# Attention with sinks and a feed-forward network on one core: the order of all engines from a list scheduler in the source, and probabilities transposed by VectorE and DMA

## The chip, the core and the metric

The kernel runs on one core of a Trainium2 chip. A core has TensorE (PE; its weight loads are shown apart as PEld), VectorE (DVE), ScalarE (ACT), GpSimd (POOL) and SyncE (SP), which here issues every DMA. Each engine executes its own instructions strictly in order and waits on semaphores for the others. The metric is the device time of one execution in microseconds; lower is better.

## The reference, cut to what matters

```python
# q, k, v: (4, 8, 768, 64); 4 sink keys, window 128; float32
scores = q @ k.T / 8
keep = is_sink | ((rel >= 0) & (rel < window))
a = softmax(where(keep, scores, -1e9))            # sum + 1e-9 in the denominator
attn = a @ v
x = attn.transpose(0, 2, 1, 3).reshape(3072, 512)
h = maximum(x @ w_in, 0)                          # w_in: (512, 2048), float64
out = (h * h) @ w_out                             # w_out: (2048, 512), float64
```

The weights come as float64 and reach the kernel as pairs of 32-bit words. `k` comes transposed, with the first eight keys appended to each block of 128 keys.

## The kernel before, in words

**Tiling.** The 3072 tokens are eight chunks of 384 (three blocks of 128 queries), two for each batch. A query block sees the key block before it, its own, and the sinks: 264 columns (128 for a batch's first block). Heads go in pairs p = 0 to 3, so there are 32 pairs, numbered s = 4c + p. The inner width of the network is cut in 16 feature blocks.

**Attention of a pair.** `score` (L251 for the first eight pairs, in float32; L255 after that, in two passes of float32r with operands made by `prep`) writes a PSUM bank s. VectorE adds the mask and takes the row's extreme in one instruction (L259, tile P, result nbs), ScalarE takes the exponential and the row sum (L262). `normalise` adds 1e-9 and takes the reciprocal (L272, L273); GpSimd multiplies the rows with it (L284) and copies the sink columns into PSK (L290, L293). From chunk 2 on GpSimd first adds the two key blocks of a row into one (L279): a column belongs to one of them by its position. `sink_keys` transposes PSK on TensorE (L300, bank pss). The probabilities are transposed on TensorE: `probs` (L335) for the first eight pairs, all ten or twelve 128x128 blocks; `probs_of` (L353) from chunk 2 on, three blocks a head, which VectorE then multiplies with the 0/1 tiles `halves` on the way to PTF (L359 to L364). `values` multiplies V with PTF and the sinks (L384, L387, bank xo) and splits the sum into a high and a low part x (L395, L396).

**The network.** `moe` runs over legs: chunk 0 and chunk 1 with feature blocks 0 to 7, then both with 8 to 15 (partial sums go through DRAM), then chunks 2 to 7 with all 16. A feature block has twelve matmuls ph (L442), three for each of the four pairs' x; the square of the positive part, split into gh and gl (L450 to L459); and nine matmuls po (L472) one block later.

**Weights.** `split_steps` turns a row of 512 float64 into a high and a low float32r part. VectorE has five passes over 512 columns (L534, L536, L538, L540, L547) and ScalarE two (L533, L546). Four rows of `w_in` hold four feature blocks together, so the first product waits for four rows. 32 rows are split in all, 16 before the second half of the blocks is needed.

**What sets the order.** For chunks 0 and 1 the text of the program does (a `manual_schedule` block: each pair's scores, the tail of the pair before, single steps of the weight rows between them as `fill`). From chunk 2 on, lists of small steps (`slot`, `values_of`) are spread evenly over the quarter steps of the products, and a tile scheduler orders the instructions within. The first pairs use two buffers for q and k in turn and two PSUM banks for attention, with others lent by name. `verdict` sums up whether the inputs lie in the range of the fast path; the flag is loaded amid the program, and `general` would run if it were set.

## Time and profile before

| | |
|---|---|
| Three runs | median 719.05 us (718.46 to 720.29) |
| Profiled execution, first to last instruction | 717.5 us (the page gives no other time of it) |
| Median of the runs above that span | 1.55 us |
| TensorE busy | 691.0 us (96%) |
| VectorE busy | 485.7 us (68%) |
| ScalarE busy | 392.4 us (55%) |
| GpSimd busy | 232.0 us (32%) |
| DMA | 71.78 MB, mean 100 GB/s |
| Chain that ended last | TensorE 87%, of it L442 35% and L472 35% |

A row of the stretches gives the stretch, its length, the busy time of each engine with the number of its instructions, the granted TensorE clock as a share, the share of DMA and GB/s. A row of the groups has line, engine, operation, tiles and shapes, then busy time and mean ns of one, then the idle time before them and who ended it. A row of the order of time has its start, its length and the merged instructions. A row of the waits has who waited for whom, the sum in us, the number of times and the longest. A row of the DMA issues has the size and the median time from issue to landing.

### The profile page before, as it was taken

How to read it: one execution, taken by the hardware profiler on the slowest of the kernel's cores; microseconds unless marked ns; L12 is line 12 of the kernel's file. 1: busy time of each engine (PE TensorE's matmuls, PEld its weight loads, DVE VectorE, ACT ScalarE, POOL GpSimd, SP SyncE). 2: the span in 40 equal slices, each digit the busy share in tenths (PEclk: the TensorE clock that was granted, in tenths of full speed). 3: DMA queues.
4: the chain of work that ended last, by engine and by line, in shares of the span. 5: the costliest groups of instructions: out<-in, count | busy, mean ns of one | idle time of the engine just before them, and what ended most of it. 6: DMA issues, size and time to landing. Idle time of an engine off the chain costs nothing.

```text
span 717.5 us, 11750 instructions
## 1 busy us (share of the span) xinstructions
PE 691.0 (96%) x3866; PEld 597.4 (83%) x3866; DVE 485.7 (68%) x1278; ACT 392.4 (55%) x1074; POOL 232.0 (32%) x432
## 2 busy tenths in 40 slices
PE   4879999999999999999999999999999999999996
PEld 2557789998878888888988888898888898889995
DVE  6887879996887776666576766766666766543222
ACT  5677666663545665666665665666566444322221
POOL 4552420042454443333244334423342424110000
PEclk9999999999999999999999999999999999999998
DMA  8465356531433522343433433334333310001001
GB/s 238 133 203 167 110 151 211 173 106 46 140 91 80 171 77 73 105 133 94 112 102 90 134 106 93 92 116 122 84 87 103 101 44 15 1 2 45 1 0 49
DMA packets 37013, 71.78 MB, mean 100 GB/s; under 512 B 4368, under 2 KB 14096, under 8 KB 36944
## 3 DMA queue, kind: packets, MB, share of 16 engines
q1 hardware_dynamic: 36944, 70.95, 33.5%
q8 instruction: 33, 0.54, 0.3%
q14 instruction: 36, 0.29, 0.2%
HBM read 63.06 MB, written 7.86 MB: 99 GB/s over the span
## 4 chain that ended last, share of the span: by engine, by line
PE 87%; DVE 6%; POOL 2%; ACT 1%; issue 1%; DMA 1%; SPq 0%; DVEq 0%; POOLq 0%; ACTq 0%
PE ph L442 35%; PE po L472 35%; PE xo L384 5%; PE s L255 4%; PE pt L353 2%; POOL P L284 1%; PE xo L387 1%; PE pss L300 1%; PE pt L335 1%; PE s L251 1%; DVE P L259 1%; ACT P L262 1%; DMA kn<-in_k_dram 1%; DVE ph L455 0%; DVE rs L272 0%
## 5 line engine op out<-in xcount | busy, mean ns | idle before, releaser
L442 PE MATMUL ph<-x,wi 128*128 128x384 f32 x1536 | 307.8, 341 | 0.0
L442 PEld LDWEIGHTS ph<-x,wi 128*128 128x128 f32 x1536 | 265.9, 188 | 8.2 <-issue 1.7
L472 PE MATMUL po<-wo,gh 128*128 128x512 f32 x768 | 243.9, 398 | 0.5 <-DVE ob L491 0.5
L223 POOL TENSOR_TENSOR KS<-kn,KS 128x408 fp32r<-128x408 f32 (+1 forms) x48 | 71.3, 1486 | 325.3 <-DVE KS L222 315.1
L472 PE MATMUL po<-wo,gl 128*128 128x512 f32 x384 | 151.4, 394 | 0.0
L472 PEld LDWEIGHTS po<-wo,gh 128*128 128x128 f32 x768 | 135.8, 188 | 18.6 <-DVE ob L491 0.8
L262 ACT ACTIVATE P<-P,nbs 128x264 f32<-128x264 f32 (+1 forms) x192 | 94.4, 492 | 85.6 <-DVE nbs L259 82.0
L450 ACT ACTIVATE r<-ph 128x384 f32<-128x384 f32 x128 | 62.7, 490 | 109.9 <-PE ph L442 109.0
L455 DVE TENSOR_TENSOR ph<-ph,r 128x384 f32<-128x384 f32 x128 | 71.6, 560 | 66.0 <-ACT r L450 65.3
L284 POOL TENSOR_SCALAR P<-P,rs 128x136 f32<-128x136 f32 (+2 forms) x192 | 82.0, 443 | 43.9 <-DVE rs L273 33.6
L472 PEld LDWEIGHTS po<-wo,gl 128*128 128x128 f32 x384 | 72.0, 188 | 16.0
L259 DVE CUSTOM_DVE_ANT_0 P<-s,maskA 128x264 f32<-128x264 f32 x128 | 53.8, 429 | 45.9 <-PE s L255 43.8
L459 DVE TENSOR_TENSOR gl<-ph,gh 128x384 fp32r<-128x384 f32 x128 | 71.0, 555 | 10.2 <-DVE ph L455 0.5
L453 ACT ACTIVATE gh<-r 128x384 fp32r<-128x384 f32 x128 | 67.1, 524 | 3.5
L255 PE MATMUL s<-KS,QS 128*128 128x264 f32 (+1 forms) x288 | 57.2, 281 | 0.9 <-DVE nbs L259 0.8
L255 PEld LDWEIGHTS s<-KS,QS 128*128 128x128 f32 x288 | 51.7, 188 | 6.6 <-DVE nbs L259 2.2
L359 DVE TENSOR_TENSOR PTF<-pt,halves 128x256 f32<-128x256 f32 x96 | 36.2, 419 | 22.9 <-PE pt L353 22.4
L272 DVE TENSOR_SCALAR rs<-sm 128x3 f32<-128x3 f32 (+1 forms) x56 | 47.3, 844 | 3.1 <-ACT P L262 1.9
L279 POOL TENSOR_TENSOR P<-P 128x256 f32<-128x256 f32 (+1 forms) x48 | 43.3, 902 | 16.7 <-ACT P L262 16.7
L384 PE MATMUL xo<-PTF,vn 128*64 128x256 f32 (+1 forms) x448 | 46.3, 347 | 0.7 <-ACT PTF L342 0.7
L384 PEld LDWEIGHTS xo<-PTF,vn 128*64 128x64 f32 x448 | 28.8, 139 | 21.8 <-issue 10.8
L395 ACT CAST x<-xo 128x384 fp32r<-128x384 f32 x32 | 15.3, 479 | 53.4 <-PE xo L387 53.4
(94 smaller groups left out, 659.9 us busy)
## 6 DMA issues: line engine op xcount, KB each, us to landing
raw<-in_moe_w_in_dram SPq DMA_DIRECT2D x16, 512.0 KB, 5.1
raw<-in_moe_w_out_dram SPq DMA_DIRECT2D x16, 512.0 KB, 3.6
half<-in_moe_w_in_dram SPq DMA_DIRECT2D x32, 256.0 KB, 3.2
half<-in_moe_w_out_dram SPq DMA_DIRECT2D x32, 256.0 KB, 3.2
kn<-in_k_dram SPq DMA_DIRECT2D x24, 272.0 KB, 4.2
qn<-in_q_dram SPq DMA_DIRECT2D x32, 192.0 KB, 3.2
out_dram<-ob SPq DMA_DIRECT2D x24, 256.0 KB, 2.3
kn<-in_k_dram SPq DMA_DIRECT2D x24, 204.0 KB, 3.7
```

What stands on the lines that cost most here:

```text
L223: nc.gpsimd.tensor_tensor(KS[:, 1, 0:nk], st["kn"][:, hh, 0:nk], f32(KS[:, 0, 0:nk]), op=ALU.subtract)
L255: nc.tensor.matmul(ps[:, 0:n], st["QS", hh][:, qcols], flat[:, a, c0 : c0 + n], start=(a == 0), stop=(a == 1))
L259: nc.vector.tensor_tensor_reduce(Pt[:, i, 0:n], ps[:, 0:n], mask[:, 0:n], -SCALE, BIG, ALU.add, ALU.min, nb)
L262: nc.scalar.activation(Pt[:, i, 0:n], Pt[:, i, 0:n], AF.Exp, bias=nb, scale=-1.0, accum_out=sm[:, i : i + 1])
L284: nc.gpsimd.tensor_scalar(Pt[:, j, 0:n], Pt[:, j, 0:n], rs[:, hh, j : j + 1], 1.0, op0=ALU.mult, op1=ALU.mult)
L384: nc.tensor.matmul(xo[h * D : h * D + D, cols], lhsT, rhs, start=(n == 0), stop=False, skip_group_check=True)
L442: nc.tensor.matmul(ph[:, 0:TOK], wi_at(i, cc, fc), xt[:, cc, :], start=(m == 0), stop=(m == 3 * NCC - 1),)
L450: nc.scalar.activation(r, ph[:, 0:TOK], AF.Relu)
L453: nc.scalar.activation(gh, r, AF.Square)
L455: nc.vector.tensor_tensor(ph[:, 0:TOK], ph[:, 0:TOK], r, op=ALU.mult)
L459: late = lambda: nc.vector.tensor_tensor(gl, ph[:, 0:TOK], f32(gh), op=ALU.subtract)
L472: nc.tensor.matmul(po[t], gt[:, ts_], wo[f][:, i, :], start=(f == f0 and j == 0), stop=(f == f1 - 1 and j == 2),)
```

## The change

**The order.** All work after the masks is put into a list of steps. Each step has an engine (or two to choose from), a duration, a rank, the steps it must follow and the PSUM banks it takes. `Plan.order` simulates the five engines: it takes again and again the step that can start first, by rank where starts are within 0.03 us, and emits it. All five engines then run in that order.

**Weights.** The two matrices are interleaved outside the kernel, so that row 2f holds the four blocks of `w_in` for feature block f and row 2f + 1 those of `w_out`. The three integer passes (L295, L302, L309) build the float32 word itself; ScalarE rounds it to the high part (L315), and the low part is a subtraction (L319), by VectorE or GpSimd.

**The first pairs.** q and k of the first eight pairs rotate over three buffers, the probabilities of the first pairs over three, PSK, SK and the transposed blocks over two each. Chunk 0 may use all eight PSUM banks. The scaling may also go to ScalarE (L527). Products are steps of three matmuls for one pair's x, so the first need only pair 0.

**Transposes from chunk 2 on.** Every row block is scaled over its 264 columns, and the addition L279 and the `halves` tiles go. VectorE transposes 32x32 blocks into T (L660, L664), four DMAs store T by partition quarters into DRAM (L677, `via`), and one DMA loads it into PT (L690), from which the value products read pieces of 32 columns. The first two chunks are still transposed by TensorE (L630).

**Smaller.** 1e-9 is added as a tile; the last output block is evacuated and stored in halves; the flag is loaded after all other work.

```diff
+class Plan:
+    HOP = 0.06
+    TAIL = {"PE": 0.17, "DVE": 0.09, "ACT": 0.11, "POOL": 0.04}
...
+    def order(self):
+        free = dict.fromkeys(("PE", "DVE", "ACT", "POOL", "SP"), 0.0)
...
+                ready, picks = self.able(s)
+                if ready is None:
+                    continue
+                e, cost, *kind = min(s["at"], key=lambda o: max(ready, free[o[0]]) + o[1] + (o[3] if len(o) > 3 else 0.0))
+                t = max(ready, free[e])
+                if e == "SP" and len(landed) > 7:
+                    t = max(t, landed[-8])
...
+                best.setdefault(e, []).append((t, s["rank"], n, cost, kind, picks))
+            chosen = None
+            for e, able in best.items():
+                first = min(able)[0]
+                a = min((a for a in able if a[0] <= first + 0.03), key=lambda a: a[1:3])
+                if chosen is None or a[0] < chosen[1][0]:
+                    chosen = e, a
...
-            nc.scalar.copy(m16[:, :, 0], words[:, :, 1])
-            nc.vector.tensor_scalar(t1, top, 3, 0x3FFFF000, op0=ALU.logical_shift_left, op1=ALU.bitwise_and)
-            nc.vector.scalar_tensor_tensor(t1, top, -0x40000000, t1, op0=ALU.bitwise_and, op1=ALU.bitwise_or)
-            nc.vector.tensor_scalar(m16[:, :, 1], words[:, :, 2], 0x1FF, None, op0=ALU.bitwise_and)
-            nc.vector.tensor_scalar(eb, t1, -0x800000, None, op0=ALU.bitwise_and)
-            nc.scalar.copy(row[:, 0, :], f32(t1))
-            nc.vector.scalar_tensor_tensor(row[:, 1, :], m, 2.0**-36, f32(eb), op0=ALU.mult, op1=ALU.mult)
+                lambda: nc.vector.tensor_scalar(
+                    f(), raw()[:, :, 1], 3, 0x3FFFFFFF, op0=ALU.logical_shift_left, op1=ALU.bitwise_and
+                ),
...
+                lambda: nc.vector.scalar_tensor_tensor(
+                    f(), raw()[:, :, 1], -0x40000000, f(), op0=ALU.bitwise_and, op1=ALU.bitwise_or
+                ),
...
+                lambda: nc.vector.scalar_tensor_tensor(
+                    f(), raw()[:, :, 0], 29, f(), op0=ALU.logical_shift_right, op1=ALU.bitwise_or
+                ),
...
+            add(("ACT", 0.52), rank, lambda: nc.scalar.copy(row()[:, 0], f32(f())), reads=[f_cell], writes=own)
...
+                vec[e].tensor_tensor(t[:, 1], f32(f()), f32(t[:, 0]), op=ALU.subtract)
...
-                if c > 1:
-                    nc.gpsimd.tensor_tensor(
-                        Pt[:, j0:NQ, 0:P], Pt[:, j0:NQ, 0:P], Pt[:, j0:NQ, BS:BAND], op=ALU.add
-                    )
...
-            for i in range(NQ):
-                nc.tensor.transpose(pt[:, i * P : (i + 1) * P], st["P"][hh][:, i, 0:P], ident)
...
+                def turn(h, which):
+                    if which == 0:
+                        dst, src = T()[:, :, 0:NQ, h], Pt(h)[:, :, BS:BAND]
+                    elif which == 1:
+                        dst, src = T()[:, :, NQ : 2 * NQ - 1, h], Pt(h)[:, 1:NQ, 0:P]
+                    else:
+                        dst, src = T()[:, :, 2 * NQ - 1, h], Pt(h)[:, 0, 0:P]
+                    if which < 2:
+                        nc.vector.transpose(
+                            dst.rearrange("p c j b -> p j c b"), src.rearrange("p j (c b) -> p j c b", b=32)
+                        )
+                    else:
+                        nc.vector.transpose(dst, src.rearrange("p (c b) -> p c b", b=32))
...
+                def put(r):
+                    nc.sync.dma_start(
+                        out=via()[:, :, r, 0:used].rearrange("c a i h b -> a c (i h b)"),
+                        in_=T()[32 * r : 32 * r + 32, :, 0:used].rearrange("a c i h b -> a c (i h b)"),
+                    )
...
+                    lambda: nc.sync.dma_start(
+                        out=PT[:, :, 0:used].rearrange("p r i h b -> p r (i h b)"),
+                        in_=via()[:, :, :, 0:used].rearrange("c a r i h b -> (c a) r (i h b)"),
+                    ),
...
+        with tc.manual_schedule(engines={E.PE, E.DVE, E.Activation, E.Pool, E.SP}):
+            for emit in plan.order():
+                emit()
```

What the lists of steps do to the order is seen at three places.

TensorE at the first product, before (names: s_c_p_h_i scores, pt transposes, xo values, ph first layer; the last pair of chunk 0 is 0_3):

```order
L335 MATMUL pt_0_3_2_584<-ident_94,P_0_3_1_414 128x128 x4
L384 MATMUL xo_0_3_605<-PTF_0_3_2_589,vn_0_3_459 64x256
L384 MATMUL xo_0_3_605<-PTF_0_3_0_561,vn_0_3_459 64x256
L384 MATMUL xo_0_3_605<-PTF_0_3_2_589,vn_0_3_459 64x256
L384 MATMUL xo_0_3_605<-PTF_0_3_0_561,vn_0_3_459 64x256
L384 MATMUL xo_0_3_605<-PTF_0_3_1_577,vn_0_3_459 64x128 x2
L387 MATMUL xo_0_3_605<-SK_140,VS_141 128x256
L442 MATMUL ph_0_0_617<-x0_0_355,wi_136 128x384 x2
L442 MATMUL ph_0_0_617<-x1_0_356,wi_136 128x384
```

and of the change (banks have numbers now; L718 and L722 are values, L770 the first layer, L630 transposes, L582 sinks; PTS belongs to pair 1, P_2 to pair 2):

```order
L718 MATMUL bank3_70<-PTS1_352,vn1_137 64x256
L718 MATMUL bank3_70<-PTS0_331,vn1_137 64x128
L722 MATMUL bank3_70<-SK_1_133,VS_126 128x256
L630 MATMUL bank5_72<-ident_78,P_2_0_224 128x128 x4
L770 MATMUL bank4_71<-x00_138,w_0_370 128x384 x2
L770 MATMUL bank4_71<-x10_139,w_0_370 128x384
L630 MATMUL bank6_73<-ident_78,P_2_0_224 128x128
L630 MATMUL bank6_73<-ident_78,P_2_1_228 128x128
L630 MATMUL bank7_74<-ident_78,P_2_1_228 128x128 x4
L582 MATMUL bank2_69<-ident_78,PSK_0_127 128x128 x2
```

The first product stood behind the values of pair 3; it now stands behind those of pair 1, ahead of pair 2's transposes.

VectorE at a row of weights, before (t1, m, eb are the passes' tiles, wi the result; SK and PTF belong to pair 0):

```order
L536 SCALAR_TENSOR_TENSOR t1_1_244<-raw_1_165,t1_1_244 128x512 [waits DVE_49]
L538 TENSOR_SCALAR m_1_245<-raw_1_165 128x512
L540 TENSOR_SCALAR eb_1_246<-t1_1_244 128x512 [waits DVE_49]
L302 CAST SK_140<-pss_0_0_272 128x256 [waits PE_49]
L340 COPY PTF_0_0_1_279<-pt_0_0_1_276 128x256 [waits PE_49]
L547 SCALAR_TENSOR_TENSOR wi_136<-m_1_245,eb_1_246 128x512 [waits DVE_49,Activation_49]
```

and of the change (f_1 and f_2 are rows 1 and 2 in work, w_0 row 0's result):

```order
L295 TENSOR_SCALAR f_1_312<-raw_1_198 128x512 [waits DMAHW1_49]
L295 TENSOR_SCALAR f_2_316<-raw_2_207 128x512 [waits DMAHW2_49]
L302 SCALAR_TENSOR_TENSOR f_1_312<-raw_1_198,f_1_312 128x512 [waits DVE_49]
L302 SCALAR_TENSOR_TENSOR f_2_316<-raw_2_207,f_2_316 128x512 [waits DVE_49]
L739 TENSOR_TENSOR x10_139<-bank4_71,x00_138 128x384 [waits Activation_49]
L309 SCALAR_TENSOR_TENSOR f_1_312<-raw_1_198,f_1_312 128x512 [waits DVE_49]
L309 SCALAR_TENSOR_TENSOR f_2_316<-raw_2_207,f_2_316 128x512 [waits DVE_49]
```

A row has three integer passes; two rows are in work at once, and a row's subtraction (L319) comes later.

TensorE in the long middle, before (chunk 5, pair 0 is transposed between the products of chunk 4):

```order
L353 MATMUL pt_5_0_0_4689<-ident_94,P_5_0_0_4424 128x128 x3
L442 MATMUL ph_4_0_4665<-x0_4_3833,wi_136 128x384 x2
L255 MATMUL s_5_1_0_1_4696<-KS_5_1_0_4531,QS_5_1_0_4532 128x264 x2
L442 MATMUL ph_4_0_4665<-x1_4_3834,wi_136 128x384
L442 MATMUL ph_4_0_4665<-x0_4_3833,wi_136 128x384 x2
L442 MATMUL ph_4_0_4665<-x1_4_3834,wi_136 128x384
L472 MATMUL po_3_0_0_3813<-wo_15_2001,gh_3_15_4646 128x512
L353 MATMUL pt_5_0_1_4712<-ident_94,P_5_0_1_4573 128x128 x3
```

and of the change, on SP, which issues the way through DRAM (pair 22; kn and qn are the loads of pairs 24 and 25):

```order
L397 DMA kn_24_4214<-in_k_dram 64x2x408
L677 DMA via_22_4246<-T_22_4164 32x4x384 [waits DVE_49]
L409 DMA vn1_137<-in_v_dram 128x512 [waits DMAHW6_49,PE_49]
L677 DMA via_22_4246<-T_22_4164 32x4x384 [waits DMAHW7_49]
L677 DMA via_22_4246<-T_22_4164 32x4x384 [waits DMAHW0_49]
L677 DMA via_22_4246<-T_22_4164 32x4x384 [waits DMAHW1_49]
L690 DMA PT_134<-via_22_4246 128x1536 [waits DMAHW5_49,DMAHW2_49,DMAHW7_49,DMAHW1_49,DMAHW0_49]
L402 DMA qn_25_4394<-in_q_dram 128x384 [waits DMAHW3_49,DVE_49]
```

The two transposing pieces on TensorE are gone; four stores and a load that waits for them stand on SP in their place, ahead of a later pair's loads.

More of the change, by code (lines that the diff above doesn't have):

```diff
@@ new lines, in attention, with turn_sinks @@
+            sk = SK[two]
+            sk_cell = "SK" if two == 0 else ("spare", 22)
+            nsq = (NQ - i0) * P
+            key = ("sk", s)
+            def turn_sinks():
+                for i in range(i0, NQ):
+                    nc.tensor.transpose(bank(key)[:, (i - i0) * P : (i - i0 + 1) * P], f32(psk[:, i]), ident)
+            r = rank(0.95)
+            add(
+                ("PE", 0.11 * (NQ - i0), 0), r, turn_sinks,
+                reads=[(psk_cell, h, *x) for h in range(2) for x in ((), (1,))] + ([] if two == 0 else [psk_cell]),
+                writes=[key], take=[("any" if early else "att", key)],
+            )
@@ L484, in evacuate @@
[L484 to L488 removed]
+            r = rank(0)
+            add(
+                ("PE", (1.08 if half == 0 else 1.3) + 0.17 + (0.175 if nsq == TOK else 0.13), 0), r, values,
+                reads=[v_cell, sk_cell, "VS"] + todo_cells[s], writes=[key_x],
+                take=[("any" if early else "att", key_x)],
+            )
@@ L740, in sink_window_attention_moe, with count @@
-        for _ in products:
-            pass
+            made["bad"] = bad
+            made["ones"] = const.tile([P, 1], F32, name="ones")
+            nc.vector.memset(made["ones"], 1.0)
+        def count():
+            nc.tensor.matmul(bank("flag")[0:1, 0:1], made["bad"], made["ones"], start=True, stop=True)
+        END = item - 6
+        add(
+            ("DVE", 2.5), END, verdict,
+            reads=["wchk"] + [("nb", s, h, i) for s in range(len(pairs)) for h in range(2) for i in range(NQ)],
+            writes=["bad"],
+        )
```

1174 lines of the change are left out of this document (656 added, 518 removed).

## The prediction

> **What bounds the kernel now.** I read the busy times of stretches of the span first, then TensorE's own order of time, then the groups of the late part. The stretches end where the stages end: TensorE's first score (4.6), the first product of the network, the end of the first leg (eight feature blocks of chunk 0), the end of the second leg, the last attention work, the last matmul.
>
> ```profile
> core 0: us, PE busy (x) PEld busy (x) DVE busy (x) ACT busy (x) POOL busy (x), PEclk, DMA share, GB/s
> 4.60:47.70 43.10, 32.32 (x161) 20.94 (x162) 36.32 (x131) 28.36 (x84) 20.70 (x42) 0.92 0.61 188
> 47.70:107.80 60.10, 57.67 (x337) 45.66 (x337) 46.61 (x121) 41.97 (x97) 21.97 (x42) 0.97 0.53 158
> 107.80:146.00 38.20, 38.20 (x195) 34.70 (x194) 37.69 (x85) 25.21 (x47) 0.00 (x0) 1.00 0.59 193
> 380.00:632.00 252.00, 252.00 (x1447) 222.23 (x1446) 169.95 (x438) 141.14 (x414) 92.37 (x166) 1.00 0.29 84
> ```
>
> From 107.8 to 711 TensorE is busy all the time; VectorE has 170 of 252 us in the long middle and nobody waits for it there. Only before 107.8 does TensorE stand still, mostly before 47.7. So there are two ways to win: less work on TensorE after 107.8, or an earlier arrival at that point. What a feature block costs TensorE stands in the undisturbed end:
>
> ```profile
> 654.70 2.08 PE ph L442 x12
> 656.78 2.06 PE po L472 x9
> ```
>
> A block is 12 plus 9 matmuls, 2.09 + 2.07 = 4.16 us, as the product alone runs there. 120 of the 128 blocks come after 107.8: 499 us. The 603 us to the end of TensorE's work therefore leave about 104 us for the 24 attention pairs of chunks 2 to 7, 4.3 us each.
>
> **Term 1: six transposes per pair leave TensorE.** L353 transposed each head in three matmuls; now VectorE turns 32x32 blocks and two DMA steps through DRAM carry the blocks to their partitions. TensorE keeps scores, sinks and values with as many columns. In order of time, a piece with a transpose and one without, at two places:
>
> ```profile
> 372.25 0.49 PE L353 MATMUL pt<-ident,P 128*128 128x128 f32 x3
> 372.49 1.29 PE L442 MATMUL ph<-x,wi 128*128 128x384 f32 x6
> 373.62 0.40 PE L255 MATMUL s<-KS,QS 128*128 128x264 f32 x2
> 373.86 1.21 PE L442 MATMUL ph<-x,wi 128*128 128x384 f32 x6
> 374.91 0.49 PE L353 MATMUL pt<-ident,P 128*128 128x128 f32 x3
> 375.15 0.71 PE L472 MATMUL po<-wo,gh 128*128 128x512 f32 x2
> 375.70 0.40 PE L472 MATMUL po<-wo,gl 128*128 128x512 f32 x1
> 375.94 0.62 PE L472 MATMUL po<-wo,gh 128*128 128x512 f32 x2
> 376.39 0.40 PE L472 MATMUL po<-wo,gl 128*128 128x512 f32 x1
> ```
>
> From start to start the three transposes take 0.24 us, and what follows them is late: six products take 1.13 instead of 1.05, two second-layer matmuls 0.55 instead of 0.45. That is 0.32 to 0.34 per head, 0.66 per pair, 24 x 0.66 = **15.8 us** off the dense part. The lower bound, without the disturbance, is 48 x 0.24 = 11.5. A pair with its four blocks then lasts 4 x 4.16 + 3.6 = 20.2 us.
>
> The cover for what replaces them is VectorE's idle third. Removed per pair are six masked copies; added are four or six block transposes, which no row shows. I bound a head's set from below by a 544-column cast and from above by the price of two 512-column passes, and take 1.5 us, nearer the upper end because the transposes read and write in pieces.
>
> ```profile
> L222 DVE CAST KS<-kn 128x544 fp32r<-128x544 f32 x24 | 10.5, 438 | 1.1 <-DMA kn<-in_k_dram 1.1
> L536 DVE SCALAR_TENSOR_TENSOR t<-raw,t 128x512 int32<-128x512 int32 x32 | 22.6, 707 | 0.2
> L359 DVE TENSOR_TENSOR PTF<-pt,halves 128x256 f32<-128x256 f32 x96 | 36.2, 419 | 22.9 <-PE pt L353 22.4
> L362 DVE TENSOR_TENSOR PTF<-pt,halves 128x128 f32<-128x128 f32 x24 | 6.7, 281 | 0.0
> ```
>
> So VectorE gains 3.0 per pair and loses about 2.2 (four at 0.42, two at 0.28): +0.8 in 20.2 us, 67% to 71% busy, free. Without that cover it would be 19 us. GpSimd loses its add (L279) and scales 264 columns instead of 136; it is busy for 92 of 252, so free too.
>
> **What could be late next** is the value product: it waits for the copy back from DRAM. In the new order the last score of a pair precedes its values by about one period, 18 to 24 us of TensorE's work. Into it must fit: reduction, exponential, reciprocal, three scalings, the second head's transposes, four stores, one load of 655 or 786 KB.
>
> ```profile
> L259 DVE CUSTOM_DVE_ANT_0 P<-s,maskA 128x264 f32<-128x264 f32 x128 | 53.8, 429 | 45.9 <-PE s L255 43.8 <-PE s L251 0.9 <-issue 0.2
> L272 DVE TENSOR_SCALAR rs<-sm 128x3 f32<-128x3 f32 x48 | 45.9, 957 | 2.8 <-ACT P L262 1.6
> L262 ACT ACTIVATE P<-P,nbs 128x264 f32<-128x264 f32 x160 | 81.6, 510 | 53.8 <-DVE nbs L259 52.2 <-POOL P L284 1.0
> L284 POOL TENSOR_SCALAR P<-P,rs 128x264 f32<-128x264 f32 x40 | 26.2, 667 | 22.3 <-DVE rs L273 18.7 <-ACT m L533 3.6
> raw<-in_moe_w_in_dram SPq DMA_DIRECT2D x16, 512.0 KB, 5.1
> kn<-in_k_dram SPq DMA_DIRECT2D x24, 272.0 KB, 4.2
> part<-ob SPq DMA_DIRECT2D x6, 256.0 KB, 2.6
> 5.87 0.90 SPq L191 DMA_DIRECT2D vn<-in_v_dram  x2
> ```
>
> The load is bounded by the 272 KB row (4.2) and by the 512 KB row scaled to 786 KB (7.8); I take 6. The stores land 2.6 after the last of four issues of 0.45, about 4.4 together. Estimate: 0.4 + 0.6 + 1.1 + 2.0 + 1.5 + 4.4 + 6 = 16.0 us, with the upper bounds 18.5. It fits into 20.2, with 4 us over; I book 0. The added traffic is 4 x 197 KB out and 786 KB back in 20 us, 78 GB/s on top of 84. The stretch 107.8:146 moved 193 with TensorE full. SP's queue is strict: the load's wait for the stores holds back the next pair's q and k, which are wanted a period later.
>
> The Trainium skill prices a DMA at 2.0 us plus bytes over 436 GB/s (DMA: Bandwidth & Descriptors, Anatomy of one DMA, a fit for transfers issued from GpSimd; these are issued from SP). By it the load would be 3.8 us and the round trip 2 to 3 us shorter, and the sum the same.
>
> **Term 2: the start.** The first product stands at 47.67, after the values of all four pairs of chunk 0, which ran one after the other:
>
> ```profile
> 7.23 0.29 DVE L259 CUSTOM_DVE_ANT_0 P<-s,mask 128x128 f32<-128x128 f32 x1
> 11.68 1.73 POOL P L284 x3
> 14.05 2.19 POOL P L284 x3
> 19.55 3.29 PE L251 MATMUL s<-kn,qn 64*128 64x128 f32 x12
> 47.67 1.22 PE L442 MATMUL ph<-x,wi 128*128 128x384 f32 x6
> 61.94 0.71 PE L251 MATMUL s<-kn,qn 64*128 64x264 f32 x4
> 62.59 1.31 PE L442 MATMUL ph<-x,wi 128*128 128x384 f32 x6
> ```
>
> Pair 2's scores wait until 19.55 for a buffer and for pair 0's six scalings on GpSimd. Now three buffers exist for q and k and three for the probabilities, eight PSUM banks are free for any use, ScalarE takes some scalings, and the first product needs one weight row and pair 0's output, not four rows and all pairs. VectorE leads to that product: its first reduction can stand near 7.2, as now. Then come 24 reductions (10 at 0.43), three rows of weights (6), the sinks, reciprocals and copies (4): 27 at most, about 25 since consecutive operations overlap a little, against 47.67.
>
> Then which engine sets the end of the leg? TensorE: 8 blocks are 33.3. A pair with 12 transposes has 6 score groups, 3 x 0.65 as at 61.94, 1.1 for transposes, 0.3 sinks, 1.7 values, some 5.1; one with 10 about 4.2. Together 37, sum 70.5, from 4.6 on: 75 at best. At the early speed it is worse: the busy time up to 107.8 was 90.0, and 4.6 + 90 = 94.6. VectorE: 36.3 + 46.6 = 82.9 busy from 4.6 on, 18 weight rows in it. A row was five passes:
>
> ```profile
> L534 DVE TENSOR_SCALAR t<-raw 128x512 int32<-128x512 int32 x32 | 14.6, 458 | 0.0
> L538 DVE TENSOR_SCALAR m<-raw 128x512 uint16<-128x512 uint16 x32 | 14.9, 465 | 0.0
> L540 DVE TENSOR_SCALAR eb<-t 128x512 int32<-128x512 int32 x32 | 14.0, 439 | 0.0
> L547 DVE SCALAR_TENSOR_TENSOR wo<-m,eb 128x512 fp32r<-128x512 int32 x16 | 11.3, 708 | 0.3
> ```
>
> With L536 that is 2.78 us. It becomes 0.46 + 2 x 0.71, and a subtraction of 0.7 that GpSimd takes for six of the first nineteen rows: 44.5 us for nineteen against 50 for eighteen. So 77.4 busy us, 82 at best. The leg ends between 82 and 95. VectorE was busy for 80% up to 107.8 and for 99% in the next leg; I take 93%, nearer to the second, because three pairs are in work at once: 4.6 + 77.4/0.93 = **88**. Gain 107.8 - 88 = 20 us, bounds 13 and 26.
>
> The second leg splits fewer rows with fewer passes than in 107.8:146, where TensorE stayed full. The end trades half a 0.68 us copy for one more store's issue; the flag's load moves behind everything, under the last store's landing. Both 0, within 1 us.
>
> **Sum.** 717.5 - 15.8 - 20 = 681.7 span. The runs' median lies 1.55 above the span (719.05 against 717.5): 683.3, say **683**.
>
> **Rivals.** First, the start stays chained: the engines wait for each other in the fixed order as they did, and the leg ends at 95 or later. For it: in that stretch GpSimd waited 30 us for reciprocals on VectorE.
>
> ```profile
> POOL P L284 <- DVE rs L273: 29.8, 6, 8.9
> ```
>
> Against: ScalarE shares that work, and buffers are three. With a leg that ends at 95 to 102 the time is 690 to 697.
>
> Second, the round trip is late. Every value product waits in TensorE's queue, and products behind it with it. From 20.2 us on, each further us costs 24. At 23 us, that is 67 us lost against 36 gained: 750, slower than before; the break-even is 21.7 us. For it: the estimate leaves only 4 us. Against: the upper bounds give 18.5. A rearranging copy could itself be far dearer: if its price were 19 times the 5.1 of the 512 KB row, one pair would take 97 us and the kernel over 2400. This is the trap that the Trainium skill names (VectorE: DVE Perf Modes, The three transpose paths): a plain DMA that transposes by strides is 19 times slower than the crossbar. It speaks of a large innermost stride; here whole runs of 1280 bytes and more are moved.
>
> Third, better than forecast: TensorE keeps its full clock from the start. The scores at 19.55 took 3.29 for six groups, those at 61.94 0.65 for two. With 75 + 3 for the leg: 673. The Trainium skill has the clock at half until one window of 3.4 us is busy (TensorE: Matmul & The Clock Gate, Part 1); by that rule denser early work pays here twice.
>
> **How the numbers follow.** Forecast 0.6, within 677 to 690. Start chained 0.18. Round trip late 0.11: a third of it still faster than before, 0.07 slower, 0.01 of it the trap. Better 0.11. The range 673 to 704 leaves out some 0.2. A difference of 0.3% (2 us) is about what a measurement of this kernel can tell. Faster is 0.6 + 0.18 + 0.11 + 0.03 = 0.92, less 0.01 for what I have not thought of; same 0.02; slower 0.07.
>
> **What would show it.** The first product near 25 us and the second leg's first one near 88; if it is above 95, term 2 failed, and the wait before the early matmuls names the engine. No transposes on TensorE after the first two chunks, and 20.2 us for four blocks and a pair; if it is 20.9, term 1 failed. The copy from DRAM landing in 5 to 8 us and no idle time of TensorE before the value products; idle time there, above all with the DMA as releaser, is the second rival. The block transposes at 0.3 to 0.7 us. The forecast is wrong outright if VectorE is above 90% busy in the long middle.

## The result and the profile after

| | before | after |
|---|---|---|
| Median of six runs each | 719.67 us (718.46 to 721.61) | 725.27 us (723.73 to 726.08) |
| Profiled span | 717.5 us | 724.3 us |
| Start of the last copy out of PSUM: first leg | 113.1 | 101.9 |
| the same, chunk 2 | 318.6 | 332.4 |
| from there to the span's end | 398.9 | 391.9 |

After to before is 1.0072, with a 95% interval from 1.0053 to 1.0092: **0.7% slower**. That is clear of the noise, but below the 2% from which two kernels are called different here. The forecast was 683, in a range from 673 to 704. The last three rows show where: the start came 11 us earlier, the stretch from the first leg to the end of chunk 2 grew from 205.5 to 230.5, and the rest is 7 us shorter. These three times are the starts of the last copy of `ob` in each leg in the order of time; that copy is what I call a leg's end below. In the changed kernel it starts 2.3 us behind the end of the first leg's last matmul (the 72nd of the second layer, 99.6), because it waits for a store that frees its buffer (VectorE's last 0.37 us before it are put down to that DMA). Where the expectations below say 101.5, they mean the boundary of the stretches, 0.4 us ahead of that copy.

The page of the changed kernel, busy times and the chain that ended last:

```profile
PE 684.0 (94%) x3722; PEld 581.9 (80%) x3722; DVE 451.8 (62%) x1207; ACT 372.1 (51%) x1058; POOL 213.6 (29%) x382
...
PE 56%; DMA 13%; DVE 13%; ACT 7%; POOL 5%; issue 4%; SPq 1%; DVEq 0%; ACTq 0%; POOLq 0%
PE bank L813 25%; PE bank L770 24%; DMA half<-in_moe_w_dram 9%; POOL P L529 4%; PE bank L481 3%; PE bank L718 3%; ACT sq L336 2%; DVE f L302 2%; DVE f L309 2%; ACT P L464 2%; DVE P L458 1%; DVE gl L799 1%; DMA part<-ob 1%; DMA out_dram<-ob 1%; DVE bank L792 1%
```

TensorE had 87% of the chain before and has 56% now. A DMA that no part of the prediction names, `half`, holds 9%. It is the load of half a weight row for the range check: in both kernels 64 such halves are loaded, squared and compared on ScalarE (`check_steps`, L331, L336, L343). The stretches of the changed kernel:

```profile
core 0: us, PE busy (x) PEld busy (x) DVE busy (x) ACT busy (x) POOL busy (x), PEclk, DMA share, GB/s
4.60:29.00 24.40, 20.06 (x106) 14.02 (x107) 19.23 (x80) 16.72 (x59) 11.62 (x23) 0.86 0.94 291
29.00:101.50 72.50, 68.36 (x414) 52.47 (x413) 69.88 (x162) 50.44 (x128) 36.69 (x57) 1.00 0.56 188
101.50:143.30 41.80, 39.19 (x199) 33.45 (x198) 40.41 (x94) 22.49 (x57) 18.20 (x22) 1.00 0.48 152
143.30:188.20 44.90, 40.84 (x209) 35.47 (x208) 26.02 (x76) 32.54 (x117) 12.61 (x24) 0.96 0.72 223
188.20:238.90 50.70, 45.46 (x257) 36.75 (x256) 31.67 (x86) 34.32 (x113) 16.27 (x30) 1.00 0.83 257
238.90:332.40 93.50, 85.24 (x451) 71.50 (x450) 52.29 (x143) 63.24 (x215) 25.00 (x48) 0.96 0.62 193
332.40:413.10 80.70, 80.60 (x451) 70.81 (x450) 52.75 (x142) 35.68 (x92) 26.99 (x48) 1.00 0.44 127
```

From 332 on TensorE is full again. Between 143 and 332 it misses 17.6 of 189.1 us, while VectorE is far from full: it waits for something else. The check's tile, first in the kernel before, then after:

```profile
L565 ACT ACTIVATE sq<-half x64: 411/418/446, 230.7 to 558.2; 128x256 bf16<-128x256 f32 x64
...
  DMA half<-in_moe_w_out_dram: 0.4, 1
...
DMA to landing us min/median/max: 2.6/3.2/4.9
```

```profile
L336 ACT ACTIVATE sq<-half x64: 409/428/442, 142.3 to 317.5; 128x256 bf16<-128x256 f32 x64
...
  DMA half<-in_moe_w_dram: 34.9, 24
...
DMA to landing us min/median/max: 2.5/3.7/6.5
```

Before, the checks stood between 230.7 and 558.2, and ScalarE waited once for a load, 0.4 us. Now they stand between 142.3 and 317.5, and ScalarE waits 24 times, 34.9 us. How this reaches TensorE, in the order of time of ScalarE and TensorE:

```profile
266.82 0.43 ACT L336 ACTIVATE sq<-half 128x256 bf16<-128x256 f32 x1 [2.47 <-DMA half<-in_moe_w_dram]
...
269.43 0.47 ACT L783 ACTIVATE r<-bank 128x384 f32<-128x384 f32 x1
269.93 0.52 ACT L787 ACTIVATE gh<-r 128x384 fp32r<-128x384 f32 x1
```

```profile
270.51 0.74 PE L813 MATMUL bank<-w,gh 128*128 128x512 f32 x2 [0.29 <-ACT gh L787]
```

ScalarE stands 2.47 us at a check. Behind it in its queue are an exponential, another check, and then the positive part r and its square gh, for which TensorE's second layer waits.

### The profile page after: what moved, and what is told of

Read it like the earlier page. It is cut to its first block, busy times and chain, and to the rows that moved or that the text cites. A ratio compares the mean times of both kernels' runs of the same rounds, so it can differ in the third digit from the quotient of the medians.

```text
span 724.3 us, 11379 instructions
## 1 busy us (share of the span) xinstructions
PE 684.0 (94%) x3722; PEld 581.9 (80%) x3722; DVE 451.8 (62%) x1207; ACT 372.1 (51%) x1058; POOL 213.6 (29%) x382
## 4 chain that ended last, share of the span: by engine, by line
PE 56%; DMA 13%; DVE 13%; ACT 7%; POOL 5%; issue 4%; SPq 1%; DVEq 0%; ACTq 0%; POOLq 0%
PE bank L813 25%; PE bank L770 24%; DMA half<-in_moe_w_dram 9%; POOL P L529 4%; PE bank L481 3%; PE bank L718 3%; ACT sq L336 2%; DVE f L302 2%; DVE f L309 2%; ACT P L464 2%; DVE P L458 1%; DVE gl L799 1%; DMA part<-ob 1%; DMA out_dram<-ob 1%; DVE bank L792 1%
## 5 line engine op out<-in xcount | busy, mean ns | idle before, releaser
L770 PE MATMUL bank<-x,w 128*128 128x384 f32 x1536 | 352.0, 341 | 0.3 <-DVE x L739 0.3
L770 PEld LDWEIGHTS bank<-x,w 128*128 128x128 f32 x1536 | 271.6, 189 | 26.7 <-issue 1.4
L813 PE MATMUL bank<-w,gh 128*128 128x512 f32 x768 | 244.2, 399 | 14.4 <-ACT gh L787 9.5
L792 DVE TENSOR_TENSOR bank<-bank,r 128x384 f32<-128x384 f32 x128 | 71.6, 560 | 168.1 <-ACT r L783 167.9
L783 ACT ACTIVATE r<-bank 128x384 f32<-128x384 f32 x128 | 62.3, 487 | 189.1 <-PE bank L770 188.8
L813 PE MATMUL bank<-w,gl 128*128 128x512 f32 x384 | 155.1, 404 | 3.3 <-DVE gl L799 2.9
L813 PEld LDWEIGHTS bank<-w,gh 128*128 128x128 f32 x768 | 138.3, 189 | 23.3 <-ACT gh L787 13.0
L529 POOL TENSOR_SCALAR P<-P,small 128x264 f32<-128x264 f32 (+1 forms) x181 | 97.6, 555 | 162.1 <-DVE small L522 143.8
L813 PEld LDWEIGHTS bank<-w,gl 128*128 128x128 f32 x384 | 72.4, 188 | 29.4 <-DVE gl L799 12.6
L799 DVE TENSOR_TENSOR gl<-bank,gh 128x384 fp32r<-128x384 f32 x128 | 70.0, 547 | 9.3 <-ACT gh L787 4.7
L660 DVE STREAM_TRANSPOSE T<-P 128x384 f32<-128x384 f32 x96 | 46.2, 496 | 25.2 <-POOL P L529 24.6
L336 ACT ACTIVATE sq<-half 128x256 bf16<-128x256 f32 x64 | 27.4, 427 | 35.5 <-DMA half<-in_moe_w_dram 34.9
L718 PE MATMUL bank<-PT,vn 128*64 128x256 f32 (+1 forms) x392 | 39.5, 341 | 0.0
L718 PEld LDWEIGHTS bank<-PT,vn 128*64 128x64 f32 x392 | 25.1, 136 | 14.7 <-issue 4.5
```

What stands on the lines that cost most here:

```text
L529: {"POOL": nc.gpsimd, "DVE": nc.vector}[engine].tensor_scalar(a, a, rs[:, h, i : i + 1], 1.0, op0=ALU.mult, op1=ALU.mult)
L718: nc.tensor.matmul(xo[h * D : h * D + D, qs[0] * P : qs[0] * P + len(qs) * P], vn[:, kk, h, :], rhs(), start=(n == 0), stop=False, skip_gr ...
L770: nc.tensor.matmul(bank(key)[:, 0:TOK], wi[fc][:, i, cc * P : (cc + 1) * P], xt[:, cc, :], start=(cc == 0 and j == 0), stop=(cc == NCC - 1 ...
L783: lambda key=key, r=r: nc.scalar.activation(r(), bank(key)[:, 0:TOK], AF.Relu),
L792: lambda key=key, r=r: nc.vector.tensor_tensor(bank(key)[:, 0:TOK], bank(key)[:, 0:TOK], r(), op=ALU.mult),
L799: lambda key=key, gh=gh, gl=gl: nc.vector.tensor_tensor(gl(), bank(key)[:, 0:TOK], f32(gh()), op=ALU.subtract),
```

## The experiments

Nine kernels whose first legs were ordered alike, the changed one among them, ended them between 100.8 and 102.7 us, so I read differences there from 2 us on.

### What the checks cost

Without them:

```diff
-                    check_steps(n, starts[g + 1] + j * (f1 - f0) / 16 if g > 3 else starts[g + 1] + j)
+        nc.gpsimd.memset(wchk, 0.0)
```

> The changed kernel without the 64 weight checks: no load of half a row, no Square and Relu on ScalarE (L331 to L343); the two check columns are set to zero instead, so the range of the weights is not tested. Theory B (the list scheduler runs the checks ahead into the stretch from 143 to 335 us, where ScalarE, strictly in order, stands at each until its load has landed, and the rectifications of the products behind it come late): the two second legs and chunk 2, together 191.6 us, lose 14 to 22 us, chunk 2 comes out at 81 to 83 like chunks 3 to 5 instead of 96, and the kernel at 703 to 711. Rival (the loss in that stretch comes from the round trip's traffic or from VectorE, and the checks only fill idle ScalarE time): chunk 2 stays above 92 and the kernel within 3 us of 725.

702.96 us; ratio to before 0.9769 (0.9732 to 0.9806). The span fell from 724.3 to 699.7, by **24.6 us** (the medians by 22.3), a little more than expected; the first leg ended at 101.2, and first leg to chunk 2 took 205.5 instead of 230.5. Theory B holds, the rival falls. One check per block instead:

```diff
+                    check_steps(n, starts[g] + j, [(("ph", c, j), NCC - 1)])   # after products(c, ...)
```

> The changed kernel with its checks kept, but each tied to one block of chunks 2 to 5: the scheduler may place the check's load only after that block's first layer, so one check goes to each block (about where the kernel before has them). Theory B: ScalarE has the time for one check per block, and the loads have landed; nearly all that is won without checks is won here too, 705 to 713. Rival (not the early and close placement but the checks themselves cost, wherever they stand): the time only moves, chunks 2 to 5 all get slower by 3 to 5 us, total within 4 us of 725.

707.29 us; 0.9823 (0.9791 to 0.9856). Most is won, but the waits were not gone: 56.0 us in 21 waits, most of them now in chunks 3 to 5; chunks 3 and 5 took 82.5 and 84.2 us instead of 80.9 and 81.0 without checks. So pacing alone was not the cure. The scheduler places a check 3.2 us behind its load's issue, and the load takes 3.7 in the median. Only that number changed:

```diff
-                ("SP", 0.4, 3.2), rank - 1,
+                ("SP", 0.4, 8.0), rank - 1,
```

> The changed kernel with one number of the scheduler changed: it reckons 8.0 us instead of 3.2 from the issue of a check's load to its landing, so a check stands later in ScalarE's order, behind work that it used to hold up; the checks are still made as early and as close together as buffers allow. Theory B, sharpened (the loss is ScalarE standing at checks whose loads take 3.7 us and more instead of the 3.2 that the order was made for): the waits of L336 for the load fall from 34.9 to below 10 us and the kernel takes 703 to 709, without any pacing. Rival (the bunching itself costs, by ScalarE's time or by 250 GB/s of traffic): 716 or more, and chunk 2 above 85.

704.21 us; 0.9773 (0.9757 to 0.979): one constant turns 0.7% slower into 2.3% faster. The check's tile in this run:

```profile
L336 ACT ACTIVATE sq<-half x64: 411/422/443, 149.1 to 451.0; 128x256 bf16<-128x256 f32 x64
...
its engine sat idle before it (us, times) until:
who waited for it (us, times):
```

No wait is left. But the number did two things: with two buffers and 8 us a load, the checks also spread to 451. Both together:

> The changed kernel with one check to a block of chunks 2 to 5 and a reckoned load time of 8.0 us. ScalarE should then wait for no check's load and have them spread as the kernel before: as without checks, 701 to 704, against 704.2 with 8.0 alone. If the spread brings nothing more: 704 to 706.

703.32 us; 0.9781 (0.9765 to 0.9797), no wait for a check's load: as without checks. Spread alone left 56 us of waits, the longer time none, with or without the pacing: the waits come from the reckoned load time.

### What the finer product steps cost

```diff
-                    for cc in range(NCC):
+                    G = NCC if c >= 2 else 1          # the nine of the second layer likewise
+                    for cc in range(0, NCC, G):
```

> The changed kernel in which from chunk 2 on the twelve matmuls of a block's first layer are one step for the scheduler, and the nine of its second layer too (the first and last block of a leg keep three steps there), as the kernel before has them, instead of groups of three that alternate. Theory C (each change between the two layers costs TensorE some 0.02 us, 0.07 per block): in chunk 7, where no attention runs, two blocks take 8.34 instead of 8.47 us, the 96 blocks give 5 to 8 us, and the kernel takes 717 to 720. Rival (what the finer steps cost in changes they win in gaps that attention would open): chunks 2 to 6 get longer by as much, time within 3 us of 725.

718.03 us; 0.9973 (0.9951 to 0.9996). The total fell as theory C wanted, but most of it elsewhere: chunk 2 fell from 88.4 to 81.0, chunks 3 to 7 together only from 385.6 to 382.0, less than the 5 to 8. Why chunk 2 gained stays open: ScalarE waited there for the checks' loads nearly as long as before (13.7 us against 16.3), but TensorE stood idle for 1.8 us instead of 5.5. With the checks paced:

> The changed kernel with one check to a block of chunks 2 to 5 (as in the run with paced checks) and the product layers of a block as whole steps from chunk 2 on (as in the run with coarse steps). If the two causes are independent: 707.3 less 3 to 5 us, 702 to 705, chunk 7 again 65.6 from last copy to last copy. If the gain of the coarse steps came only from where they put the checks: 706 to 709.

716.27 us; 0.9954 (0.9937 to 0.9971), neither of the two. Chunks 3 to 5 took 85.0, 86.4 and 84.0, and the waits for the loads were back:

```profile
  DMA half<-in_moe_w_dram: 79.8, 32
...
DMA to landing us min/median/max: 2.5/4.5/6.6
```

With the longer load time the two are separate:

> The reckoned load time of 8.0 us together with whole product layers as steps from chunk 2 on. If the two causes add up, and the loss of the earlier pair (paced checks with coarse steps, 716) was again ScalarE standing at loads (60 us of waits between 310 and 560): 699 to 705. If coarse steps disturb for another reason: 708 or more, chunks 3 to 5 at 83 and above.

705.43 us; 0.9779 (0.9758 to 0.98). Chunks 3 to 7 took 382.8 against 385.8 with fine steps, **3.0 us** in 80 blocks. TensorE's order of time in chunk 7 gives a block of 4.18:

```profile
661.36 2.27 PE L771 MATMUL bank<-x,w 128*128 128x384 f32 x12
...
665.54 2.27 PE L771 MATMUL bank<-x,w 128*128 128x384 f32 x12
...
669.72 2.27 PE L771 MATMUL bank<-x,w 128*128 128x384 f32 x12
```

The total gained nothing: the second leg of chunk 1 took 51.9 instead of 48.9. Theory C is right in kind and worth 3 us.

### What the transposes were worth

Three transposes of a constant ahead of each head's first scores, in the kernel without checks:

```diff
+                        for _ in range(NQ if i == 0 else 0):
+                            nc.tensor.transpose(bank(key)[:, 384:512], ident, ident)
```

> The kernel without checks (703.0 us) with three TensorE transposes of a constant put ahead of the first score group of each head from chunk 2 on, into an unused piece of that bank; the path through VectorE and the DMAs stays, and every order is unchanged. It pays the removed TensorE work alone: 144 transposes. By the prediction's price (0.66 per pair with the disturbance): chunks 3 to 6 get longer by 2.6 us each and the kernel by 14 to 16. By the undisturbed price (0.24 per head): 2 us each, 11 to 12 in all. If other waits cover it: less than 8.

715.49 us in one run; span 713.6 against 699.7, **13.9 us** for 24 pairs, 0.58 a pair. Of this, 1.2 us stand in the first leg, before the added transposes, and are noise. Chunks 3 to 5 grew by 2.3, 2.5 and 2.5, which is 0.61 a pair.

### What bounds the first leg

An integer pass of the rows (L309) left out, the order made anew:

> The changed kernel with one of the three integer passes of every weight row left out (the one at L309, so the lowest bits of the weights are missing): 32 VectorE passes of 0.75 to 0.85 us fewer, 22 of them before 101.5 us. Theory A (VectorE is the bound up to 143 us): the end of the first leg moves from 101.5 by two thirds or more of 17 us, to 84 to 91, the second leg takes 34 to 38 instead of 41.8, and the kernel 702 to 714. Rival (the early part hangs on the chain through scores, exponentials and GpSimd, or on TensorE's own order, and VectorE only looks full): the first leg ends within 4 us of 101.5 and the kernel at 719 or more.

719.32 us; 0.9998 (0.9974 to 1.0022). The first leg ended at 100.5: theory A seemed to fall. But the scheduler had filled VectorE again: 28 rows' second passes stood before 100 us, against 23 before 101.5 in the changed kernel. A run that lets the scheduler reorder does not measure one engine. So the next ones keep every order. First more work for TensorE:

```diff
-                        for h, kk, qs, off in blocks:
+                        for h, kk, qs, off in 2 * blocks:
```

> The changed kernel in which every TensorE transpose of the probabilities in the first two chunks is issued twice (88 more of them, the same result; every engine's order otherwise unchanged, since the scheduler's costs are). Theory D (TensorE itself bounds the first leg: between 29 and 101.5 us it is busy for 94%, and a pair of the first two chunks costs it some 6.8 us and not the 4.6 of the prediction): the first leg ends later by most of the 88 x 0.11 = 10 us, at 108 to 112. Theory A (VectorE bounds the leg, 96% busy): the additional transposes fall into TensorE's waits, and the leg ends by at most 4 us later, at 101 to 106.

730.63 us in one run; the first leg at 104.4, 2.5 later. Theory D falls. With L309 in the plan and only its instruction left out:

```diff
-                lambda: nc.vector.scalar_tensor_tensor(
-                    f(), raw()[:, :, 0], 29, f(), op0=ALU.logical_shift_right, op1=ALU.bitwise_or
-                ),
+                lambda: None,
```

> The changed kernel with the integer pass at L309 left out of every weight row as in the earlier run (the lowest bits of the weights are missing), but with the pass still in the scheduler's plan, so that every engine's order is that of the changed kernel and nothing moves into the freed time. 22 passes of 0.75 us less on VectorE before 101.5. Theory A: the first leg ends 8 us or more earlier, 93 or less. Theory D: it ends at 97 to 102. For the second leg (VectorE 97% busy there, and TensorE's waits are for gl) both expect 37 to 40 instead of 41.8.

710.08 us in one run; the first leg ended at **93.2**, 8.7 earlier, as theory A said, though for 17 us of work that is half. The second leg took 41.0 between last copies against 43.7, less of a gain than both theories expected. Gating the late rows:

> The changed kernel with paced checks, in which the sixteen weight rows of the second half of the network (needed from 143 us on) may be loaded only once given blocks of the first two legs are done (four within blocks 4 to 7 of the first leg, the others two to a block of the second), so that they can't run ahead. Theory A' (the rows that run ahead stand in VectorE's order before what the first leg's products need): the first leg ends at 96 or earlier. Theory D: it ends within 3 us of 101.5. The second leg: 38 to 44, since the rows then stand there.

708.63 us in one run, the first leg at 101.6: the rows that run ahead are not the cause. Then the other engines got more work, each in an unchanged order, in one run each (737.48, 740.20 and 732.16 us):

> The changed kernel with the first integer pass of each weight row (L295) issued twice, same result, every order unchanged: 22 x 0.45 = 9.9 us more on VectorE before the end of the first leg. VectorE bounds the leg: it ends 7 to 10 us later, 109 to 112. No single engine does (a chain that passes from queue to queue): 2 to 6 us later, 104 to 108.

> The changed kernel with the two operations on GpSimd that pick out the sink columns (L542, L544) issued twice in the first two chunks, same result, every order unchanged: 12.1 us more on GpSimd, which is 50% busy there. VectorE bounds the leg: it ends within 2 us of 101.9. The chain from probabilities over GpSimd to TensorE's transposes bounds it (6.9 us of TensorE's waits there are for GpSimd): 5 us later or more.

> The changed kernel with ScalarE's rounding of each weight row (L315) issued twice, same result, every order unchanged: 22 x 0.62 = 13.5 us more on ScalarE, which is 69% busy in the first leg. VectorE bounds the leg: it ends within 3 us of 101.9. ScalarE stands in the chain: 5 us later or more.

| instructions doubled on | added busy us up to that end | first leg's end | later by |
|---|---|---|---|
| GpSimd (L542, L544) | 10.2 | 116.0 | 14.1 |
| VectorE (L295) | 11.7 | 110.3 | 8.4 |
| ScalarE (L315) | 13.6 | 107.4 | 5.5 |
| TensorE (L630) | 9.7 | 104.4 | 2.5 |

The added times are measured; the expectations had reckoned 12.1 for GpSimd and 9.9 for VectorE. VectorE's row came out as if it bounded the leg, but so did GpSimd's, which is busy for half of the time, and ScalarE's reached the 5 us that stood for the chain. TensorE, 94% busy, counts least. TensorE's waits up to 116 us in the run with GpSimd's sink steps doubled:

```profile
PE bank L582 <- POOL PSK L542: 10.6, 5, 3.4
PE bank L475 <- DMA kn<-in_k_dram: 5.0, 2, 4.5
PE bank L630 <- POOL P L529: 4.4, 6, 1.9
```

In the changed kernel the first row is 3.2 us. TensorE's granted clock was lower as well: 0.86 from 29 to 101.5 us, against 1.00. That may be why more was lost than added, but no run separates the two. A stretch of that run, and the same of the changed kernel:

```profile
40.00:50.00 10.00, 10.00 (x50) 6.93 (x49) 7.29 (x21) 6.73 (x21) 4.71 (x13) 0.73 0.49 143
```

```profile
40.00:50.00 10.00, 9.66 (x64) 6.61 (x60) 9.96 (x29) 8.82 (x27) 4.88 (x10) 1.00 0.51 167
```

So no single engine bounds the leg. That it hangs on a chain of probabilities (VectorE's reciprocals, GpSimd's scalings and sink pieces, TensorE's transposes) is read from the waits; no run cuts this chain at one link. GpSimd's groups in the changed kernel, first from 29 to 101 us, then from 300 to 600:

```profile
L529 POOL TENSOR_SCALAR P<-P,small 128x264 f32<-128x264 f32 x22 | 14.2, 659 | 11.1 <-DVE small L522 7.1 <-PE bank L770 4.0
...
L544 POOL CAST PSK<-P 128x48 fp32r<-128x48 f32 x8 | 3.9, 496 | 0.0
L542 POOL TENSOR_TENSOR PSK<-P,PSK 128x24 fp32r<-128x24 f32 x8 | 3.7, 472 | 0.2
```

```profile
L529 POOL TENSOR_SCALAR P<-P,small 128x264 f32<-128x264 f32 x72 | 36.9, 526 | 80.7 <-DVE small L522 80.7
...
L542 POOL TENSOR_TENSOR PSK<-P,PSK 128x24 fp32r<-128x24 f32 x14 | 3.3, 239 | 1.2
...
L544 POOL CAST PSK<-P 128x48 fp32r<-128x48 f32 x14 | 3.1, 224 | 0.4
```

Beside a VectorE that is 96% busy, mostly with row passes, the sink steps of chunk 1's pairs took twice as long as later, and the scalings a quarter more; the smaller sink steps of chunk 0 took 204 and 234 ns in this window, as later (209 and 222), but 290 and 295 over the whole leg. The scheduler reckons 0.46, 0.29 and 0.32 for them everywhere. (The Trainium skill, SBUF — State Buffer, SBUF: two separate sides, says that a GpSimd operation that reads SBUF and a VectorE operation with two SBUF inputs lock each other out for a whole instruction; L302, L309 and L319 have two. The longer steps agree, but no run here isolates the lock.) Two runs moved the rows' subtraction between GpSimd and VectorE:

```diff
-LOW_DVE = 0.3
+LOW_DVE = 9.0      # first run: low parts on GpSimd; -9.0 in the second: on VectorE
```

> The reckoned load time of 8.0 us, and the last subtraction of every weight row always on GpSimd (penalty for GpSimd's alternative raised from 0.3 to 9): 13 subtractions of 0.79 us fewer on VectorE between 29 and 101.5, 19 more of 1.47 us on GpSimd up to 143. By the run with the omitted pass in an unchanged order (17 us off VectorE moved the first leg's end by 8.7): the first leg ends 4 to 5 us earlier, at 97, and the kernel takes 4 us less than the run with 8.0 alone. Rival (as in the run with the omitted pass in a new order, the scheduler fills VectorE with rows that are needed later, or GpSimd now delays the scalings): the first leg at 100 or later.

714.61 us; 0.9923 (0.9901 to 0.9946); first leg at 106.3, 4.6 later than with 8.0 alone, although 14 subtractions had left VectorE. The rival's side, and more: the work went to where it costs more, and VectorE's own passes grew longer. Before 101.5 us, L295, L302 and L309 took 714, 884 and 736 ns with 21 subtractions on GpSimd; 453, 788 and 761 with eight (8.0 alone); 436, 703 and 718 with none (the next run). So the row passes on VectorE cost more, the more of the subtractions GpSimd takes. The next run starts from the kernel with paced checks and 8.0:

> The same kernel with the last subtraction of every weight row always on VectorE: before 101.5 some eight of 1.47 us fewer on GpSimd, eight of 0.79 more on VectorE. By the measured slopes (GpSimd 14.1 per 12.1, VectorE 8.4 per 9.9) the first leg ends 13.6 earlier and 5.4 later, about 8 earlier, at 93, if the slopes hold for less work as for more. If only work in the chain itself counts (scalings and sink steps, not the rows' subtraction): 2 to 5 us later, 103 to 106.

701.76 us; 0.9747 (0.9695 to 0.98); first leg at 99.0 instead of the 101.3 of that kernel: the direction of the slopes, a third of their size, so they don't hold for less work as for more. Last, the durations alone, in the same kernel:

```diff
-                        pool = ("POOL", 0.46 if n > P else 0.33)
+                        pool = ("POOL", (0.62 if n > P else 0.6) if plain else 0.46 if n > P else 0.33)
-                            ("POOL", 0.29), r - URGE + 0.01, lambda h=h: part_sinks(h, False),
+                            ("POOL", 0.45 if plain else 0.29), r - URGE + 0.01, lambda h=h: part_sinks(h, False),
...
-                ("DVE", 0.345, "port"), rank,
+                ("DVE", 0.42, "port"), rank,
```

> The kernel with paced checks and a reckoned load time of 8.0 us (703.3 us, first leg ends at 101.3), in which the scheduler also reckons with the durations that the first leg shows: scalings on GpSimd 0.62 and 0.6 us instead of 0.46 and 0.33, the two sink steps 0.45 each instead of 0.29 and 0.32 (first two chunks), the rows' passes on VectorE 0.42 and 0.7 instead of 0.345 and 0.6, the low part 0.7 or 1.47. If the first leg is lost to steps that come later than the order reckons, as with the checks: it ends at 93 to 98 and the kernel takes 697 to 701. If it is lost to the amount of work on engines that hold each other up: within 2 us of 101.3 and 703.3.

**696.78 us; 0.9686 (0.9647 to 0.9726)**: the fastest kernel here, 3.1% below the kernel before. The first leg ended at 94.5 instead of 101.3. Its stretches:

```profile
4.60:29.00 24.40, 19.43 (x124) 13.46 (x124) 21.49 (x89) 20.43 (x71) 7.92 (x22) 1.00 1.02 304
4.60:101.50 96.90, 90.73 (x548) 69.73 (x549) 90.12 (x252) 72.72 (x203) 29.07 (x60) 1.00 0.68 215
101.50:143.30 41.80, 41.47 (x216) 36.97 (x215) 41.01 (x95) 21.00 (x51) 9.96 (x15) 1.00 0.51 157
```

With the corrected prices the scheduler gave ScalarE and VectorE steps that it had given GpSimd: from 4.6 to 101.5 GpSimd is busy for 29.07 us instead of 48.11 in the kernel that this run starts from. The first product stands at 21.6 instead of 28.5, and the clock of the first stretch is 1.00 instead of 0.86. How much of the 7 us is the shift of work and how much the better order was not separated.

## Why the prediction was wrong

Forecast for the span 681.7, measured 724.3: 42.6 us too much. The runs account for 40.2 of them; each row compares single profiled executions, and executions of one kernel lie 2 to 3 us apart:

| | us | from |
|---|---|---|
| ScalarE waiting for the checks' loads | 24.6 | span with and without checks |
| First leg 11.9 us earlier instead of 20 | 8.1 | the mark below, before and without checks |
| Finer product steps | 3.0 | chunks 3 to 7, fine against coarse steps |
| TensorE idle in the second leg | 2.6 | 39.19 of 41.80 us busy; without checks also 2.6 idle |
| Transposes worth 13.9 instead of 15.8 | 1.9 | transposes put back |

The mark: the forecast's 107.8 and 88 are the moment at which TensorE begins the second layer of the first leg's last block. Before, and in the changed kernel:

```profile
107.83 0.63 PE L472 MATMUL po<-wo,gh 128*128 128x512 f32 x2
```

```profile
96.75 0.63 PE L813 MATMUL bank<-w,gh 128*128 128x512 f32 x2
```

So the changed kernel is 11.1 us earlier and 8.8 behind the forecast; without checks the mark is at 95.9. The last copies say the same (113.1, 101.9 and 101.2). The prediction also calls 107.8 the second leg's first product. That one stood at 105.8 and now stands at 95.2, just above the 95 that was named as the sign of a failed term 2.

**The step that failed first** is one not taken. The sum carries "From 107.8 to 711 TensorE is busy all the time" over to the new order, and behind the first leg it books nothing but the transposes. The prediction counts rows, transposes and the round trip there and leaves out the 64 checks, which the scheduler also moved, from 230.7:558.2 to 142.3:317.5, past the products on ScalarE's queue, with their loads on SP's. ScalarE stood at them for 34.9 us, and the kernel lost 24.6. The checks' own work cost nothing that shows (703.3 with all of them spread and never waited for, 703.0 without); the price was the wait at the head of a strict queue. None of the rivals had it, so the range was too short above.

**Term 2, the first leg: wrong in size, with an end in the first rival's range.** The first product came at 29.0 (25 forecast). The step that failed is the sum by VectorE's busy time, "4.6 + 77.4/0.93 = 88". The share was right, 92% up to the mark, but VectorE was busy for 84.6 us there and not 77.4: L302 and L309 took 0.79 and 0.76 where 0.71 was taken, the low part 0.76 instead of 0.7, and 22 rows stood there instead of the nineteen counted. With 84.6 the sum gives 95.6, near the measured 96.8. That does not make VectorE the bound: the table of added work shows that no one engine was. The rival "the start stays chained" puts the end at 95 to 102, and 96.8 lies there, but the wait that it names as evidence, GpSimd's for reciprocals, had shrunk from 29.8 to 10.7 us. TensorE's 70.5 for the leg was too low as well: up to the mark it was busy for 83.7, where the kernel before had 90.0. With corrected durations the mark is at 90.2, still short of 88. And the second leg, booked with 0, left TensorE idle for 2.6 us.

**Term 1, the transposes: right, a little high.** 0.66 a pair forecast, 0.58 measured with the transposes put back (0.61 in chunks 3 to 5), between the lower bound (0.48) and the value taken. A pair with its four blocks takes 20.4 us from values to values (20.2 forecast):

```profile
406.92 1.52 PE L718 MATMUL bank<-PT,vn 128*64 128x256 f32 x16
427.34 1.52 PE L718 MATMUL bank<-PT,vn 128*64 128x256 f32 x16
447.80 1.52 PE L718 MATMUL bank<-PT,vn 128*64 128x256 f32 x16
```

The 0.2 more fit the finer steps, 3.0 us in 80 blocks: 0.04 a block, 0.15 for four.

**The round trip and its cover: right.** No wait of TensorE for PT stands among the changed kernel's waits, and VectorE is 65% busy from 332.4 to 413.1 (67% to 71% forecast). The loads over the whole execution, and the block transposes from 300 to 600 us:

```profile
PT<-via SPq DMA_DIRECT2D x12, 768.0 KB, 5.4
PT<-via SPq DMA_DIRECT2D x12, 640.0 KB, 5.3
```

```profile
L660 DVE STREAM_TRANSPOSE T<-P 128x384 f32<-128x384 f32 x29 | 16.8, 578 | 21.5 <-POOL P L529 21.0 <-DMA out_dram<-ob 0.4
L660 DVE STREAM_TRANSPOSE T<-P 128x256 f32<-128x256 f32 x29 | 12.2, 419 | 0.0
L664 DVE STREAM_TRANSPOSE T<-P 128x128 f32<-128x128 f32 x14 | 4.0, 285 | 0.0
```

The load landed in 5.3 to 5.4 over the whole execution (6 taken, 5 to 8 as the sign) and in 4.3 to 4.7 from 300 to 600 us; a head's transposes take 1.0 to 1.3 (1.5 taken). The prediction's 18.5 for the round trip's upper bounds does not follow from its terms: with 7.8 for the load they give 17.8. Nothing hangs on it. The second rival, with its trap, did not happen. By the fit that the prediction cites from the Trainium skill (DMA: Bandwidth & Descriptors, Anatomy of one DMA) the load would be 3.8; the row decides, 5.4. The third rival's full clock came only with corrected durations: 1.00 from 4.6 to 29 us, against 0.86 in the changed kernel.

**The end** cost what was booked: from the last copy to the span's end 6.3 us against 6.5 before.

## What to carry to other kernels

A strict queue makes an early, unimportant step dear if what it waits for comes later than reckoned (here 3.7 us in the median and up to 6.5, against 3.2). Before pricing what a scheduler gains, list every kind of step that it moved, and for each that waits on a DMA compare the reckoned time with the slowest landing, not the median. A list scheduler's constants are part of the kernel: load time and durations corrected from rows of its own trace, with the checks paced, were worth 28 us here, twice the transposes. To find what bounds a stretch in which several engines look full, add a known amount to one engine at a time without changing the order; taking work away under a scheduler that may reorder answers another question.

## What the runs showed of the hardware

- The same 256 KB load from DRAM landed in 3.2 us (median) in the kernel before, 3.7 in the changed one, 4.1 and 4.5 with the checks paced (fine, coarse steps), with a spread from 2.5 to 6.6 among these: the median alone is no safe distance.
- GpSimd's sink steps of chunk 1 doubled in length beside a busy VectorE (496 against 224 ns, 472 against 239), while the 264-column scaling grew by a quarter (659 against 526). The other way round, VectorE's pass L295 took 714 ns with 21 subtractions on GpSimd, 453 with eight and 436 with none (three runs whose orders differ).
- Alternating three matmuls of one layer with three of the other costs TensorE about 0.04 us a block of 21 matmuls against whole layers (385.8 against 382.8 us for 80 blocks, granted clock 1.00).
- With GpSimd's sink steps doubled the granted clock was 0.73 between 40 and 50 us (1.00 in the changed kernel), and 10.2 us of added work made 14.1 of delay. Whether the clock made the difference is not shown.
